# Attention and two expert layers in one kernel: where the later experts' raw weights are put and when their loads are issued, and 512-wide dummy matmuls

## The chip, the cores and the metric

The kernel runs on one core of a Trainium2 chip. The metric is the device time of one execution in microseconds (us), lower is better. Every engine of the core runs its own list of instructions in order: TensorE (PE, matmuls; PEld are its weight loads), VectorE (DVE), ScalarE (ACT), GpSimd (POOL) and SyncE (SP, which issues most transfers). They meet at semaphores.

## What is computed

A recurrence over 768 steps for 4 x 8 heads, whose output becomes 3072 rows of 384; a dense layer with leaky ReLU; then a layer of eight experts, of which each row uses at most one:

```
state = w * state + outer(k_t, v_t)              # attention, per head
y[t]  = r_t @ (state_before + outer(u * k_t, v_t))
x = leaky(y @ w_in) @ w_out                      # 3072 x 384 -> 2048 -> 384
do = x @ w_skip > 0                              # only these rows are changed
e  = argmax(x @ w_gate); gate = softmax(x @ w_gate)[e]
out[do] = x + gate * (relu(x @ w1[e]) @ w2[e])   # 384 -> 1024 -> 384
```

## The kernel before

Everything is written out by hand in one order (the recording layer keeps the order of the calls), so each engine's list is the order of the code. Each weight matrix is used as a high and a low float16 part; a product is three matmuls.

**Head.** The string SEQ names the steps of the attention, the conversion of the dense layer's weights and its first matmuls, one letter each. The letter W is a dummy matmul, 256 columns wide, that writes a bank nobody reads; there are 38 more before the string and 2 after each of the four steps at L181. After SEQ come the groups of the dense layer. They end at about 511 us of the span.

**Experts.** They are numbered 0 to 7, so the first, third and fifth are numbers 0, 2 and 4. A block is 128 rows of one expert: POOL gathers the rows (`gather`, L659), SP turns them with a DMA transpose (`turn_rows`, L673, into a tile xT, or into consts), PE runs 72 matmuls of `hidden` (L981 to L983) and 24 of `combine` (L997 to L999), DVE writes y (L1001), POOL scatters y into the output (L1004). Expert 1's first block comes first of all; then the loop L1045 goes through the experts. The numbers of rows are known only at run time, so each block after the first stands in a branch (`tc.If`), and `announce` (L1021) tells the engines' instruction fetch which way it will go. The blocks of expert 1 after its first are called block 1, 2 and 3 here.

**Weights.** An expert's split weights fill one of five slots; expert e uses slot e mod 5 of D, E, A, B, C (L681). The raw float32 weights come from HBM in eight pieces of 384 KB: four of w1 (0 to 3), four of w2 (4 to 7). `load_pieces(n)` issues the next n loads on SP (L697), always into eight places of the tile raw; `split_pieces(n)` makes the two parts of the next n pieces, ACT the high one (L190) and DVE the low one (L191), and after each, unless state["hold"] is set, loads one more piece. PIECES says how many pieces an expert's first block splits: 2, 1 and 3, at three places of it, but 2 for expert 1. So an expert splits pieces of the next one or two and loads pieces about an expert further on. The list `later` (L841) is the order of the loads.

**Expert 1's last block.** Its rows come by `fetch(e, 3)`, which stands at the head of block 1 (L1063 to L1065): on POOL and SP it comes after all that L1047 to L1050 issue, that is the fetch for expert 2, the fetch for expert 3 (into consts) and the loads that go with two splits. The matmuls of block 3 wait for this tile, xT of buffer 6.

Of the kernel before, what the change touches and what calls it, by code (L numbers as in the profile page):

```python
# [9 lines left out]
F32 = mybir.dt.float32  # L10
# [8 lines left out]
P = 128  # L19
NB, H, S, D = 4, 8, 768, 48  # L20
NT, DM, DFF = 3072, 384, 2048
E, F2 = 8, 1024
# [20 lines left out]
NW = 8  # L43
# [4 lines left out]
W0 = 30  # L48
W1 = 2
SEQ = "UqcaAWWWsDLnWWWWWWWWWWspLUqWWWWWvycNTBCWWWWWWrXLLdBqpCLtWWWWWWWWWWWWWvaueXByTlCnWWWWWWWsXWWWWrcTDpaBCWWWWWWWWWWWWWWWWWvulyXtLlBLCLqheLXLBCnXhWWWWWWWWWWWWWWWWWWWWWWWsBrtchdWWWWvCXBCepqWWWWWWWWWWWWWWWWWWWWWWWWWyluXTWWWWWrBCXBNllLCaWWWWWmLXAkvLcmuTeKmsBmcCkmdkXBsDnhkphCmmkqLpXByhCXhLkTWWWWWWWWWvBLCXLuyBCmnXBrtmtKmkLLeTmrehLCkmhvcXBlkCmKmmKLkmkaXBdmKilKmmkCmKXBCmmKlqkskXmLBmCumKkxhXBLCmmnKkXBjlmpkxmkCLKLxqmmmhXByCvxlT2KXT2BLCxXx2BLClacrLedXLfLa2q2BClXhBsx2x2lLpUCXhxB2CXBfCXyhBT2kCxxlXn2BC2xalcxrXLB2ChXxf2xl2x2s2kTq"  # L50
NB2 = 7
E0 = 1
# [8 lines left out]
def kernel(ctx: ExitStack, tc: tile.TileContext, rk, nat, wT, uN, w_in, w_out, wsg,  # L61
                         w1, w2, c_diag, c_mask, c_id48, c_f16, c_route, c_tok, out):
    nc = tc.nc
    v, act, g_, pe, sp = nc.vector, nc.scalar, nc.gpsimd, nc.tensor, nc.sync
# [14 lines left out]
    bank = [psp.tile([P, 512], F32, name=f"bank{i}") for i in range(8)]  # L79
    turns = {}  # L80
    steps = {}
    state = {"ring": 3, "loads": 0, "seq": True, "done": 0, "hold": False}
# [10 lines left out]
    wu = cst.tile([P, 2 * P], F16, name="wu")  # L93
# [5 lines left out]
    def whole():  # L99
        last_rows.clear()  # L100

    def warm(n, b, w=2 * P):

        for _ in range(n):
            whole()
            pe.matmul(bank[b][:, 256:256 + w], wu[:, :P], wu[:, :w], start=True, stop=True)


    for b in range(4):
        for o in (0, 256):  # L110
            whole()
            pe.matmul(bank[b][:, o:o + 256], wu[:, :P], wu, start=True, stop=True)
    warm(W0, 5)


    def att_load():
# [35 lines left out]
    slotA = slots.tile([P, 2, NK, DFF], F16, name="slotA")  # L152
    slotB = slots.tile([P, 2, NF, WX], F16, name="slotB")
    slotC = slots.tile([P, 2, NF, GT], F16, name="slotC")
    slotD = slots.tile([P, 2, NF, GT], F16, name="slotD")
# [22 lines left out]
    for p in range(NPAIR):  # L178
        for o in (0, 64):
            for q in range(2):  # L180
                pe.matmul(bank[q][o:o + C, p * D:(p + 1) * D], ltab[64 * q:64 * q + D, p, :], id48[64 * q:64 * q + D, :],  # L181
                          start=True, stop=True)
        warm(W1, 5)
    for q in range(2):
        act.copy(lnat[:, q].rearrange("a b c -> a (b c)"), bank[q][:, :NPAIR * D])

# [2 lines left out]
    def split(hi, lo, src, sc, eng=None):  # L189
        act.activation(hi, src, AF.Copy, scale=sc)  # L190
        (eng or v).scalar_tensor_tensor(lo, src, sc, hi, op0=ALU.mult, op1=ALU.subtract)  # L191
# [461 lines left out]
    def buf_of(e, j):  # L653
        return 3 * (e % 2) + j if j < 3 else 6
# [28 lines left out]
    def expert_piece(e, c):  # L683

        w1s, w2s = ev[e % len(ev)]
        if c < 4:
            n = F2 // 4
            sl = slice(c * n, (c + 1) * n)
            return w1[e, :, :, sl], w1s[:, 0, :, sl], w1s[:, 1, :, sl], NK
        sl = slice(2 * c - 8, 2 * c - 6)  # L690
        return w2[e, :, sl, :], w2s[:, 0, sl, :], w2s[:, 1, sl, :], 2

    def load_expert(e, c, pool, bufs):
        src, hi, lo, n = expert_piece(e, c)
        t = pool[c] if isinstance(pool, list) else pool.tile([P, 768], F32, name="wst", bufs=bufs)
        t3 = t.rearrange("p (a b) -> p a b", a=n)
        sp.dma_start(t3, src)  # L697
        return lambda eng=None: split(hi, lo, t3, SW, eng)
# [90 lines left out]
    def first_post(eng):  # L789
        turn("k")  # L790
        posts.pop(0)(eng)
# [4 lines left out]
             "q": att_load, "L": load_w, "B": conv_a, "C": conv_b, "X": conv_d,  # L796
             "l": lambda: conv_low(v), "h": lambda: conv_low(g_), "x": turn_w_out, "m": first_mm1, "M": lambda: first_mm1(g_), "2": first_mm2,
             "k": lambda: first_post(g_), "K": lambda: first_post(v), "f": first_fuse, "i": init_loads, "j": init_routing,
             "W": lambda: warm(1, 4 + (turns.get("mm", -1) + 1) % 3)}
    for x in SEQ:  # L800
        order[x]()
    state.update(ring=4, seq=False)
    turns["mm"] = 2
# [34 lines left out]
        take_logits(0, pl, 1.0 / (SX * SR))  # L838

    w_b = [raw[:, i * 768:(i + 1) * 768] for i in range(NW)]  # L840
    later = [(e, c) for e in range(2, E) for c in range(8)]  # L841
    parts = []

    def load_pieces(n):
        for _ in range(min(n, len(later))):
            parts.append(load_expert(*later.pop(0), w_b, NW))

    def split_pieces(n, more=True):
        for _ in range(min(n, len(parts))):
            parts.pop(0)()  # L850
            if more and not state["hold"]:
                load_pieces(1)
# [118 lines left out]
    def hidden(e, k, par, hset, cuts=(0, 0), between=None):  # L971
        w1s, _ = ev[e % len(ev)]
        xT = xT_b[k]
        h = h_b[par]
        for b in range(2):
            hp = hps[hset][b]
            for f in range(4):
                fs = slice((4 * b + f) * P, (4 * b + f + 1) * P)
                o = hp[:, f * P:(f + 1) * P]
                for c in range(NK):  # L980
                    pe.matmul(o, w1s[:, 0, c, fs], xT[:, c, :], start=c == 0, stop=False)  # L981
                    pe.matmul(o, w1s[:, 0, c, fs], xT[:, NK + c, :], start=False, stop=False)
                    pe.matmul(o, w1s[:, 1, c, fs], xT[:, c, :], start=False, stop=c == NK - 1)  # L983
            split_pieces(cuts[b])
            hh = h[:, 0, 4 * b:4 * b + 4, :].rearrange("p a b -> p (a b)")
            hl = h[:, 1, 4 * b:4 * b + 4, :].rearrange("p a b -> p (a b)")
            act.activation(hh, hp, AF.Relu)  # L987
            v.scalar_tensor_tensor(hl, hp, 0.0, hh, op0=ALU.max, op1=ALU.subtract)  # L988
            if between and b == 0:
                between()  # L990
# [24 lines left out]
    def fetch_ahead(e):  # L1015
        if e < E:
            fetch(e, 0)

    def announce(e, j, engines=ENGINES):

        tc.mark_branch_hint_location(f"e{e}b{j}", (rv[e] + (NT + 1023 - j * P)) >> 12, engines=engines)  # L1021
# [3 lines left out]
    def fetch_more(e):  # L1025
        with tc.If(rv[e] > P):  # L1026
            fetch(e, 1)
            with tc.If(rv[e] > 2 * P):  # L1028
                fetch(e, 2)

    def passage():
        turn_here(0, 0, bank[0])
        next(cnts)
        fetch_more(E0)
        fetch_more(0)
        state["hold"] = False
        load_pieces(2)

    state["hold"] = True
# [5 lines left out]
    for e in range(E):  # L1045
        odd = 1 if e == E0 else 0
        if e == E0:  # L1047
            fetch_more(e + 1)
            fetch_ahead(e + 2)
            split_pieces(sum(PIECES[e + 1]))  # L1050
        else:
            announce(e, 1)
            cuts = PIECES[e + 1]
            hidden(e, buf_of(e, 0), e % 2, e % 2, cuts[:2], lambda: announce(e, 1, ENGINES[:1]))
            split_pieces(cuts[2])
            announce(e, 1, ENGINES[:1])
            if e + 1 < E and e + 1 != E0:
                fetch_more(e + 1)
            combine(e, buf_of(e, 0), e % 2, idx_t[:, 0, e:e + 1], lambda: fetch_ahead(e + 2))
        st = ExitStack()  # L1060
        for j in range(1, NBLK):
            st.enter_context(tc.If(rv[e] > j * P, label=f"e{e}b{j}"))
            if j == 1:  # L1063
                with tc.If(rv[e] > 3 * P):  # L1064
                    fetch(e, 3)  # L1065
            announce(e, j + 1)
            hidden(e, buf_of(e, j), (e + j + odd) % 2, 2 if (j + odd) % 2 else e % 2, (0, 0),
                   lambda: announce(e, j + 1, ENGINES[:1]))
            announce(e, j + 1, ENGINES[:1])
            combine(e, buf_of(e, j), (e + j + odd) % 2, idx_t[:, j, e:e + 1])  # L1070
        with tc.If(rv[e] > NBLK * P, label=f"e{e}b{NBLK}"):  # L1071
            nb = (rv[e] + (P - 1)) // P
            k = NB2 - 1
            with tc.For_i(NBLK, nb, 1) as jb:
                for i in range(TPG):
                    sp.dma_start(idx_l[:, i:i + 1], idxl[i][bass.ds(jb * P + e * NT, P), :])
                v.tensor_reduce(idx_m, idx_l, op=ALU.min, axis=AX.X)
                fetch(e, 0, k, idx_m)
                hidden(e, k, e % 2, e % 2)
                combine(e, k, e % 2, idx_m)  # L1080
        st.close()  # L1081
    with tc.If(rv[E] > 0):
        later[:] = [(E0, c) for c in range(8)]
        load_pieces(8)
        idx_f = m2p.tile([P, 1], U32, name="idxf")
        v.tensor_scalar(idx_f, steps["early_i"], NT, 4 * NT, op0=ALU.is_lt, op1=ALU.mult)
        v.tensor_max(idx_f, idx_f, idx_t[:, 0, E0:E0 + 1])
        fetch(E0, 0, None, idx_f)
        split_pieces(8)
        hidden(E0, k0, 0, 2)  # L1090
        combine(E0, k0, 0, idx_f)
# [80 lines left out]
```

## Time and profile before

| | us |
|---|---|
| median of 3 runs (649.68 to 653.81) | 651.92 |
| the profiled execution | 653.15 |
| its span, first to last instruction | 651.0 |
| PE busy | 606.3 (93%) |
| DVE busy | 420.2 (65%) |
| ACT busy | 255.9 (39%) |
| POOL busy | 253.7 (39%) |
| mean granted TensorE clock | 0.987 |

A share of busy time is a mean over the whole span. PE is the engine that is nearly always at work; what it waits for decides, and only those waits of PE that a change moves can move the end. In the rows, "PEq" is PE's own sequencer, which runs branches and fetches instructions; a wait that ended with PEq ended with a branch. SPq and POOLq are transfers that SP and POOL issue: the time beside them is that of the issue, not of the transfer.

### The profile page before, as it was taken

To read this page: it belongs to the slowest core of one execution; us is meant where nothing else is said; L and a number is where in the kernel's file an instruction comes from. 1 tells how busy PE (TensorE), PEld (TensorE's weight loads), DVE (VectorE), ACT (ScalarE), POOL (GpSimd) and SP (SyncE) were. 2 spreads that over 40 slices of the span, in tenths; PEclk is the share of its full clock that TensorE was granted. 3 is DMA by queue.
4 is the path that set the end of the run, shared out by engine and by line. 5 is a ranking of instruction groups with operands and counts; after the bars stand their busy time and mean duration, and the time that the engine had idled before them with its cause. 6 is when DMAs were issued, how large, how long until landed. Compare 5 with 4: busy or idle time off the path is not lost. (4 is left out here: it accounts for less than half of the span.)

```text
span 651.0 us, 17764 instructions
## 1 busy us (share of the span) xinstructions
PE 606.3 (93%) x7198; PEld 404.4 (62%) x7198; DVE 420.2 (65%) x915; ACT 255.9 (39%) x539; POOL 253.7 (39%) x242
## 2 busy tenths in 40 slices
PE   8889988889999999999999999999998888989894
PEld 6666555556666666656666666665665666777673
DVE  6899988953379559858965961861577262553751
ACT  1226656552145235434533621441454141432540
POOL 3867764543544622534553261430024122221210
PEclk9989999999999999999999999999999899989997
DMA  8767354623624552562553242021366498397930
GB/s 262 233 186 224 95 169 138 188 66 75 161 89 127 147 187 66 135 185 78 147 150 117 65 100 87 2 74 34 110 177 193 147 224 209 94 195 200 191 135 12
DMA packets 60350, 89.04 MB, mean 137 GB/s; under 512 B 20706, under 2 KB 44224, under 8 KB 60240
## 3 DMA queue, kind: packets, MB, share of 16 engines
q1 hardware_dynamic: 56784, 81.64, 45.2%
q0 software_dynamic: 2880, 5.49, 2.8%
q8 instruction: 66, 1.08, 0.7%
q10 hardware_dynamic: 576, 0.47, 0.2%
q14 instruction: 44, 0.36, 0.2%
HBM read 68.86 MB, written 17.23 MB: 132 GB/s over the span
## 5 line engine op out<-in xcount | busy, mean ns | idle before, releaser
L476 PE MATMUL bank<-xt,slotA 128*128 128x384 f16 x384 | 125.6, 327 | 2.4 <-DVE gg L482 2.3
L478 PE MATMUL bank<-xt,slotA 128*128 128x384 f16 x384 | 125.4, 326 | 0.0
L477 PE MATMUL bank<-xt,slotA 128*128 128x384 f16 x384 | 125.3, 326 | 0.0
L504 PE MATMUL bank<-slotB,slotC 128*128 128x393 f16 (+1 forms) x336 | 110.7, 329 | 0.0
L506 PE MATMUL bank<-slotB,slotC 128*128 128x393 f16 (+1 forms) x336 | 110.5, 329 | 0.0
L505 PE MATMUL bank<-slotB,slotC 128*128 128x393 f16 (+1 forms) x336 | 110.5, 329 | 0.0
L482 DVE TENSOR_TENSOR gg<-bank,gg 128x384 f32<-128x384 f32 x128 | 70.0, 550 | 29.4 <-ACT gg L481 28.9
L481 ACT ACTIVATE gg<-bank 128x384 f32<-128x384 f32 x128 | 62.1, 490 | 48.8 <-PE bank L478 46.4
L492 DVE TENSOR_TENSOR slotC<-gg,slotC 128x384 f16<-128x384 f32 x101 | 77.7, 773 | 0.2
L297 POOL TENSOR_TENSOR dg<-cs,diag 128x512 f32<-128x512 f32 x21 | 22.2, 1058 | 131.8 <-DVE cs L290 131.8
L491 ACT CAST slotC<-gg 128x384 f16<-128x384 f32 x112 | 56.8, 508 | 22.5 <-DVE gg L482 22.5
L532 DVE SCALAR_TENSOR_TENSOR x<-bank,x 128x384 f16<-128x384 f32 x24 | 13.2, 556 | 71.4 <-ACT x L529 71.4
L269 POOL TENSOR_TENSOR raw<-raw,consts 112x512 f32<-112x512 f32 x44 | 56.9, 1318 | 0.0
L477 PEld LDWEIGHTS <-slotA 128*128 128x128 f16 x384 | 37.6, 98 | 25.1 <-issue 3.2
L478 PEld LDWEIGHTS <-slotA 128*128 128x128 f16 x384 | 37.6, 98 | 25.0 <-issue 0.2
L476 PEld LDWEIGHTS <-slotA 128*128 128x128 f16 x384 | 37.6, 98 | 23.9 <-issue 0.2
L528 ACT ACTIVATE x<-bank 128x384 f16<-128x384 f32 x24 | 11.8, 493 | 99.2 <-PE bank L506 81.2
L506 PEld LDWEIGHTS <-slotC 128*128 128x128 f16 x336 | 32.9, 98 | 22.7
L504 PEld LDWEIGHTS <-slotC 128*128 128x128 f16 x336 | 32.8, 98 | 21.9
L505 PEld LDWEIGHTS <-slotC 128*128 128x128 f16 x336 | 32.9, 98 | 20.8
L987 ACT ACTIVATE h<-bank 128x512 f16<-128x512 f32 x28 | 16.7, 597 | 71.5 <-PE bank L983 57.3
L988 DVE SCALAR_TENSOR_TENSOR h<-bank,h 128x512 f16<-128x512 f32 x28 | 19.4, 691 | 38.0 <-ACT h L987 34.0
(212 smaller groups left out, 1312.2 us busy)
## 6 DMA issues: line engine op xcount, KB each, us to landing
raw<-in_w SPq DMA_DIRECT2D x48, 384.0 KB, 6.6
raw<-in_nat SPq DMA_DIRECT2D x24, 576.0 KB, 5.4
raw<-in_rk SPq DMA_DIRECT2D x24, 448.0 KB, 4.3
xbuf<-x SPq DMA_DIRECT2D x23, 384.5 KB, 6.3
wst<-in_w_in SPq DMA_DIRECT2D x16, 384.0 KB, 7.6
wst<-in_w_out SPq DMA_DIRECT2D x16, 384.0 KB, 3.6
wst<-in_w SPq DMA_DIRECT2D x16, 384.0 KB, 5.9
out_x<-x SPq DMA_DIRECT2D x24, 192.0 KB, 1.9
```

Source lines behind the costliest of these rows:

```text
L269: eng.tensor_mul(r4[:, a], r4[:, a], tab.unsqueeze(2).broadcast_to([112, NPAIR, 2, C]))
L297: eng.tensor_mul(dg, steps.pop(("cs", i)).unsqueeze(3).broadcast_to([P, 2, NPAIR, C]), diag.unsqueeze(1).unsqueeze(1).broadcast_to([P, 2, ...
L476: pe.matmul(ph[:, :n], wh, xt[:, 0, k, t0:t0 + n], start=k == 0, stop=False)
L477: pe.matmul(ph[:, :n], wh, xt[:, 1, k, t0:t0 + n], start=False, stop=False)
L478: pe.matmul(ph[:, :n], wl, xt[:, 0, k, t0:t0 + n], start=False, stop=k == NK - 1)
L481: act.activation(gg[:, :n], ph[:, :n], AF.Copy, scale=0.01)
L482: v.tensor_max(gg[:, :n], ph[:, :n], gg[:, :n])
L491: act.copy(gT[:, 0, f, t0:t0 + n], gg[:, :n])
L492: eng.tensor_sub(gT[:, 1, f, t0:t0 + n], gg[:, :n], gT[:, 0, f, t0:t0 + n])
L504: pe.matmul(po[:, :c1 - c0], gh, w_out_s[:, 0, f, c0:c1], start=start, stop=False)
L505: pe.matmul(po[:, :c1 - c0], gh, w_out_s[:, 1, f, c0:c1], start=False, stop=False)
L506: pe.matmul(po[:, :c1 - c0], gl, w_out_s[:, 0, f, c0:c1], start=False, stop=stop)
```

## The change

Three things change.

1. A dummy matmul can be 512 wide: it reads the 256 columns of wu twice and writes a whole bank. The dummies before SEQ, those at L181 and pairs of W ahead of SEQ's first m become half as many of double width.
2. The list `later` says for each piece where it lands. Pieces 2 to 7 of expert 4 land in slot D, which expert 0 has used; all of expert 6 land in slot A, which expert 2 has used; the rest in raw. Experts 5 and 7 load (and split) pieces 2 to 7 first and 0 and 1 last.
3. Splits load nothing until expert 3's first block. Instead there are three calls of load_pieces: 10 in expert 1, 4 ahead of expert 2's first block, 8 ahead of expert 3's. As the loop goes, the loads issued in each expert's turn are:

| turn of expert | 0 | 1 | 2 | 3 | 4 | 5 |
|---|---|---|---|---|---|---|
| loads before (2 ahead of expert 0) | 6 | 2 | 6 | 6 | 6 | 4 |
| loads now (2 ahead of expert 0) | 0 | 10 | 4 | 14 | 2 | 0 |

```diff
+            if w > 2 * P:
+                pe.matmul(bank[b], wu[:, :P], wu.unsqueeze(1).broadcast_to([P, 2, 2 * P]), start=True, stop=True)
+                continue
...
-    warm(W0, 5)
+        warm(1, b, 4 * P)
+    warm(W0 // 2, 5, 4 * P)
...
-        warm(W1, 5)
+        warm(W1 // 2, 5, 4 * P)
...
-    for x in SEQ:
+    head, tail = SEQ[:SEQ.index("m")], SEQ[SEQ.index("m"):]
+    for x in head.replace("WW", "w") + tail:
...
-    later = [(e, c) for e in range(2, E) for c in range(8)]
+    rest = [2, 3, 4, 5, 6, 7, 0, 1]
+    store = {e: t.rearrange("p a b c -> p (a b c)")[:, :8 * 2 * 768].bitcast(F32) for e, t in ((4, slotD), (6, slotA))}
+    store = {e: [t[:, i * 768:(i + 1) * 768] for i in range(8)] for e, t in store.items()}
+    later = ([(e, c, w_b) for e in (2, 3) for c in range(8)] + [(4, c, w_b) for c in (0, 1)]
+             + [(4, c, store[4]) for c in range(2, 8)] + [(5, c, w_b) for c in rest]
+             + [(6, c, store[6]) for c in range(8)] + [(7, c, w_b) for c in rest])
...
         fetch_more(E0)
         fetch_more(0)
-        state["hold"] = False
         load_pieces(2)
...
             fetch_ahead(e + 2)
             split_pieces(sum(PIECES[e + 1]))
+            load_pieces(10)
         else:
             announce(e, 1)
             cuts = PIECES[e + 1]
+            if e == 2:
+                load_pieces(4)
+            if e == 3:
+                load_pieces(8)
+                state["hold"] = False
             hidden(e, buf_of(e, 0), e % 2, e % 2, cuts[:2], lambda: announce(e, 1, ENGINES[:1]))
```

What this moves on SP is seen at two places. The first is expert 1's turn, from the transpose for expert 3 (consts) to the one for expert 1's block 3 (xT_6535 before, xT_6453 now, the same buffer 6; both read its rows xg). Before:

```order
L673 DMA_TRANSPOSE consts<-consts 128x6x128
L697 DMA raw<-in_w 128x3x256 x2
L1081 COMPARE_AND_BRANCH
L1064 COMPARE_AND_BRANCH
L673 DMA_TRANSPOSE xT_6535<-xg_6534 128x6x128
L1064 UNCONDITIONAL_BRANCH x2
```

Now:

```order
L674 DMA_TRANSPOSE consts<-consts 128x6x128
L698 DMA slotD<-in_w 128x3x256 x2
L698 DMA slotD<-in_w 128x768 x4
L698 DMA raw<-in_w 128x3x256 x2
L698 DMA raw<-in_w 128x768 x2
L1093 COMPARE_AND_BRANCH
L1076 COMPARE_AND_BRANCH
L674 DMA_TRANSPOSE xT_6453<-xg_6452 128x6x128
L1076 UNCONDITIONAL_BRANCH x2
```

Ten loads stand between the two transposes where two stood. The second place is the head of expert 0's turn, between the branches of the passage and the transpose for expert 2 (xT_6520 before, xT_6438 now). Before:

```order
L697 DMA raw<-in_w 128x3x256 x2
L1021 ISA
L1168 BRANCH_PREFETCH_HINT
L697 DMA raw<-in_w 128x3x256 x2
L697 DMA raw<-in_w 128x768 x4
L673 DMA_TRANSPOSE xT_6520<-xg_6519 128x6x128
```

Now:

```order
L698 DMA raw<-in_w 128x3x256 x2
L1028 ISA
L1180 BRANCH_PREFETCH_HINT
L674 DMA_TRANSPOSE xT_6438<-xg_6437 128x6x128
L1093 COMPARE_AND_BRANCH
```

Six loads have left the place ahead of that transpose.

## Rows read from the trace of the kernel before

**Rows 1.** The page, part 1: busy us (share) and instructions of each engine.
```profile
PE 606.3 (93%) x7198; PEld 404.4 (62%) x7198; DVE 420.2 (65%) x915; ACT 255.9 (39%) x539; POOL 253.7 (39%) x242
```

**Rows 2.** Timeline of DVE, experts, lines L1001: start us, us, then the instruction.
```profile
550.68 0.62 DVE L1001 SCALAR_TENSOR_TENSOR y<-bank,xg 128x384 f32<-128x384 f32 x1 [2.60 <-PE bank L999]
...
561.23 0.62 DVE L1001 SCALAR_TENSOR_TENSOR y<-bank,xg 128x384 f32<-128x384 f32 x1 [2.60 <-PEq L1071]
...
570.01 0.61 DVE L1001 SCALAR_TENSOR_TENSOR y<-bank,xg 128x384 f32<-128x384 f32 x1
...
581.66 0.61 DVE L1001 SCALAR_TENSOR_TENSOR y<-bank,consts 128x384 f32<-128x384 f32 x1
...
589.52 0.62 DVE L1001 SCALAR_TENSOR_TENSOR y<-bank,xg 128x384 f32<-128x384 f32 x1 [2.60 <-DMA out_x<-y,idx]
...
606.40 0.62 DVE L1001 SCALAR_TENSOR_TENSOR y<-bank,xg 128x384 f32<-128x384 f32 x1
```

**Rows 3.** Waits of PE at 533, 549, 560, 569, 597, 606 us: total, times, longest.
```profile
PE bank L981 <- issue: 1.2, 1, 1.2
...
PE bank L981 <- DMA xT<-xg: 2.3, 1, 2.3
...
PE bank L981 <- PEq L1071: 0.6, 1, 0.6
...
PE bank L981 <- PEq L1081: 1.9, 1, 1.9
...
PE bank L981 <- PEq L1081: 0.7, 1, 0.7
...
PE bank L981 <- PEq L1081: 2.2, 1, 2.2
```

**Rows 4.** Windows: busy PE, PEld, DVE, ACT, POOL (instructions); clock, DMA share, GB/s.
```profile
572.00:576.00 4.00, 4.00 (x47) 4.00 (x44) 0.98 (x2) 0.77 (x2) 1.55 (x1) 0.57 1.55 265
...
642.00:651.00 9.00, 0.00 (x0) 0.00 (x0) 0.29 (x1) 0.00 (x0) 0.97 (x1) 0.62 0.04 15
```

**Rows 5.** Timeline of SP, experts: start us, us of issuing, transfer, number issued.
```profile
528.04 5.86 SPq L697 DMA_DIRECT2D raw<-in_w  x8
541.46 1.26 SPq L673 DMA_TRANSPOSE xT<-xg  x1
544.69 1.24 SPq L673 DMA_TRANSPOSE consts<-consts  x1
546.04 1.26 SPq L697 DMA_DIRECT2D raw<-in_w  x2
548.14 1.23 SPq L673 DMA_TRANSPOSE xT<-xg  x1
563.40 7.05 SPq L697 DMA_DIRECT2D raw<-in_w  x6
...
582.19 5.06 SPq L697 DMA_DIRECT2D raw<-in_w  x6
...
599.63 7.30 SPq L697 DMA_DIRECT2D raw<-in_w  x6
```

**Rows 6.** Timeline of POOL, the gathers for expert 2, expert 3 and block 3.
```profile
534.26 1.03 POOL L659 DMA_INDIRECT xg<-xbuf,idx  x1 [8.49 <-DVEq L1081]
...
538.25 1.02 POOL L659 DMA_INDIRECT consts<-xbuf,idx  x1 [1.09 <-DMA raw<-in_w]
...
544.22 1.00 POOL L659 DMA_INDIRECT xg<-xbuf,idx  x1 [4.95 <-SPq L1081]
```

**Rows 7.** Transfers issued in 528:534, 546:548, 544:546: number, KB, median us to landing.
```profile
raw<-in_w SPq DMA_DIRECT2D x8, 384.0 KB, 8.3
...
raw<-in_w SPq DMA_DIRECT2D x2, 384.0 KB, 4.9
...
xg<-xbuf,idx POOLq DMA_INDIRECT x1, 3.9
```

**Rows 8.** Window of the dummies L106 alone: PE busy (matmuls), PEld, clock, DMA, GB/s.
```profile
6.00:7.40 1.40, 1.40 (x15) 1.25 (x14) 1.00 1.10 347
```

More of the change, by code (lines that the diff above doesn't have):

```diff
@@ L105, in warm @@
             whole()
+            if w > 2 * P:
+                pe.matmul(bank[b], wu[:, :P], wu.unsqueeze(1).broadcast_to([P, 2, 2 * P]), start=True, stop=True)
+                continue
             pe.matmul(bank[b][:, 256:256 + w], wu[:, :P], wu[:, :w], start=True, stop=True)
     for b in range(4):
-        for o in (0, 256):
-            whole()
-            pe.matmul(bank[b][:, o:o + 256], wu[:, :P], wu, start=True, stop=True)
-    warm(W0, 5)
+        warm(1, b, 4 * P)
+    warm(W0 // 2, 5, 4 * P)
     def att_load():
@@ L798 @@
              "k": lambda: first_post(g_), "K": lambda: first_post(v), "f": first_fuse, "i": init_loads, "j": init_routing,
-             "W": lambda: warm(1, 4 + (turns.get("mm", -1) + 1) % 3)}
-    for x in SEQ:
+             "W": lambda: warm(1, 4 + (turns.get("mm", -1) + 1) % 3), "w": lambda: warm(1, 4, 4 * P)}
+    head, tail = SEQ[:SEQ.index("m")], SEQ[SEQ.index("m"):]
+    for x in head.replace("WW", "w") + tail:
         order[x]()
@@ L845, in load_pieces @@
         for _ in range(min(n, len(later))):
-            parts.append(load_expert(*later.pop(0), w_b, NW))
+            parts.append(load_expert(*later.pop(0), NW))
     def split_pieces(n, more=True):
@@ L1082 @@
     with tc.If(rv[E] > 0):
-        later[:] = [(E0, c) for c in range(8)]
+        later[:] = [(E0, c, w_b) for c in range(8)]
         load_pieces(8)
```

## The prediction

> **What bounds the kernel now.** I read the page's busy shares first: PE works 93% of the span, the next engine 65% [rows 1]. So time is lost or won where PE stands still, and an edit that touches no such place costs nothing. The change leaves the dense layer alone; it alters the dummies of the head and the stretch of the experts. There I read the timeline of DVE, whose y marks the end of each block. A block that waits for nothing lasts 589.52 - 581.66 = 7.86 us [rows 2]; what an interval has beyond that is loss. Then the waits of PE by windows [rows 3] say what ended the loss. Four of them matter here:
>
> - Expert 1's block 3 (y 550.68 to 561.23): PE waits 2.3 us for its tile xT.
> - End of expert 2 (y 570.01 to 581.66, 11.65 us): a wait of 1.9 us that ended with PE's own sequencer, at a branch. The remaining 11.65 - 7.86 - 1.9 = 1.9 us has its cause in the window 572 to 576: granted clock 0.57 on average, that is mostly 1.2 GHz instead of 2.4, with PE busy throughout [rows 4], right behind the wait.
> - End of expert 4, behind the y at 606.40: a wait of 2.2 us on the sequencer.
> - For comparison, the same kind of wait is 0.6 us at the end of expert 1 and 0.7 us at the end of expert 3 [rows 3].
>
> What distinguishes the long branches from the short ones is seen on SP [rows 5]: six loads are issued from 563.40 in expert 2 and six from 599.63 in expert 4, each burst running over the branch; at the ends of experts 1 (about 561) and 3 (about 597) the last loads were issued by 547.3 and 587.3, ten microseconds and more earlier. I read this as: the code behind the branch is itself a transfer and arrives late when weight loads fill the DMA engines. Expert 0 speaks half against it: eight loads from 528.04, and a wait of 1.2 us put down to issue, not to the sequencer.
>
> The chain behind the 2.3 us of block 3 is longer. The gather for expert 2 goes out at 534.26 [rows 6], among eight loads, and SP can issue its transpose only at 541.46, 7.2 us later; a gather with few loads beside it lands in 3.9 [rows 7]. SP goes on in order: the transpose for expert 3 at 544.69, two loads at 546.04, block 3's transpose at 548.14 [rows 5]. POOL's gather for block 3 itself waited 4.95 us for SP until 544.22 [rows 6]. The transpose landed when PE's wait ended, 550.6 + 2.3 = 552.9.
>
> **The dummies: nothing.** In the window 6.0 to 7.4 the dummies keep PE busy without a hole, 15 of them in 1.4 us [rows 8]; half as many of double width are the same columns. From both sides: if every merged pair saved a tenth of its length, about 0.01 us for some 80 pairs, -0.8; if each real matmul behind a wide dummy started 0.1 us later at some ten places, +1. I take 0 since no idle time lies between them.
>
> **Expert 0's six loads gone.** Its own branch needs nothing from this: the 1.2 us are issue. I count 0. What it does is to bring SP forward. The gather for expert 2 then lands at 534.26 + 3.9 = 538.2, so its transpose is issued 3.3 us sooner. The gather for expert 3, issued at 538.25, lands at about 542.2, and its transpose goes out there instead of at 544.69. By itself this would take away block 3's wait.
>
> **Expert 1's ten loads: the term that decides.** They stand on SP between the transpose for expert 3 and the one for block 3, where two stood. SP issues a load in 0.63 us (two in 1.26 [rows 5]). First load: 542.2 + 1.3 = 543.5. Tenth: issued before 550. All go through the one hardware queue of SP, and so does block 3's transpose behind them. How long it stands behind them I take from two rows. Two loads landed 4.9 us after issue; of eight loads issued in 5.86 us the median took 8.3 [rows 7]. The eighth was issued at about 533.2 and so landed at about 541.5, the first at about 528.04 + 4.9 = 532.9: 8.6 / 7 = 1.23 us per load. Ten loads then land until 543.5 + 4.9 + 9 x 1.23 = 559.5. The transpose came 1.3 us behind the last load in front of it before (546.7 + 4.9 = 551.6, then 552.9): 560.8. PE finishes block 2 at 550.6 as now, so it waits 10.2 us instead of 2.3: **+7.9**. Bounds: if the loads land as fast as they are issued, 543.5 + 4.9 + 9 x 0.63 + 1.3 = 555.4, that is +2.5; if the ten, a gather, a scatter and a transpose (4.7 MB in all) move at the 265 GB/s of the crowded window in [rows 4], 17.8 us from 544.7 on and 1.3 more, 563.8, that is +10.9. I take +7.9, nearest to the row with eight loads.
>
> A rule to weigh against this: the Trainium skill, "DMA: Bandwidth & Descriptors", section Bandwidth, gives about 358 GB/s as a core's share of HBM. By it, nine further loads of 0.393 MB take an estimated 9.9 us instead of 11.1, and the term would be +6.7; no window read here reaches that rate.
>
> After ten idle microseconds the clock falls: at the end of the kernel PE does nothing from 642 to 651, and that window has 0.62 [rows 4]. Block 3 then begins at the lower clock. The price of one such stretch is the 1.9 us measured above: **+1.9** (bounds 0 and twice that). While PE waits, nothing else suffers: ACT and DVE have only splits to do, and the loads wait for none of PE's later work. POOL's scatters come later by the same amount, with PE.
>
> **Expert 2's four loads.** They are issued ahead of its splits, right after block 3's transpose, and with the delay above they have landed before its branch. So its end becomes one like expert 1's: 1.9 to 0.6, **-1.3**, and the half clock behind it goes with the wait, **-1.9**. Bounds: 0 and -3.2.
>
> **Expert 3's fourteen, expert 4's two, expert 5's none.** At expert 4's end two loads instead of six are in front: 2.2 to 0.6, **-1.6** (bounds -1.6 and 0, since expert 3's loads may still run). Fourteen loads at 1.23 fill 17 us of expert 3's three blocks (24 us), and its rows were fetched in expert 2's turn; its end may become a long branch (+1.5) or not. I take 0, because the last block announces its branch a whole block earlier. Splitting pieces 0 and 1 of expert 7 last puts them just ahead of its first matmuls; DVE has finished such splits at the y of the block before [rows 2], where PE only begins the next: 0.
>
> **Sum.** +7.9 + 1.9 - 1.3 - 1.9 - 1.6 = **+5.0 us**. The profiled execution took 653.15 (span 651.0 and 2.15 around it), which makes 658.2; it stands 1.2 above the median 651.92, so in the measure of the median **656.9 us**, 0.8% slower. Its own range, from the bounds: 649.6 (+2.5, no clock loss) to 663.
>
> **Rivals.**
>
> 1. Block 3 is not late (chance 0.15). For it: SP and POOL reach it 3 us sooner, and a transpose might not wait for loads that stand in front of it. Then the 2.3 us stay or go, with the gains kept: -4.8 to -7.1, **647.1 down to 644.8**. It decides if the transpose lands before 552.9. Against it: loads took 8.3 instead of 4.9 us where eight stood together, and it is the same queue. The Trainium skill, "DMA: Bandwidth & Descriptors", section Queues, rings and completion order, says that each DMA engine takes descriptors in ring order but that completions may overtake one another; the first half is my forecast, the second is this rival, and no row here shows one.
> 2. The long branches are not due to the loads, or move to the end of expert 3 (0.2). For it: expert 0's branch among loads was short. Then only +7.9 + 1.9 stays, **661.7**, slower by 1.5%.
> 3. The loads hide in both places and nothing measurable moves, as all engines but PE have room (0.1): **652**. Against it: the waits above are PE's own.
>
> **Chances.** My forecast has 0.55. A difference of 1%, 6.5 us, is about what a measurement of this kernel can tell from no change. Slower by more than that is above 658.4: a third of the forecast (the upper half of the bounds of the ten loads) and rival 2, 0.39. Faster is below 645.4: only rival 1 with its whole gain, 0.06. The rest, 0.55, is within 1%. The range that holds 8 in 10 leaves out the best of rival 1 and the ends of the forecast: 647 to 663.
>
> **What would show it.** In the profile after: the wait of PE for xT before block 3 of expert 1 about 10 us instead of 2.3, with SP's ten loads from about 543.5 and block 3's transpose issued after 550; the granted clock low behind it; the waits at the ends of experts 2 and 4 at 0.6 to 0.7, and the stretch behind expert 2 at full clock. A wait under 3 us at block 3 makes the forecast wrong; long branches at experts 2 and 4, or a new one at the end of 3, put rival 2 in its place.

## The result and the profile after

The changed kernel takes 661.13 us (median of 4 runs, 658.57 to 661.30), the kernel before beside it 650.93 (4 runs, 649.68 to 653.81). The ratio is 1.0118, 95% interval 1.0084 to 1.0151: slower by 1.2%. The forecast was 656.9, in a range of 647 to 663. The profiled execution took 661.19 us with a span of 659.0, 8.0 more than before.

The page's shares look as they did [rows 1]:

```profile
PE 608.3 (92%) x7116; PEld 395.1 (60%) x7116; DVE 418.5 (64%) x915; ACT 255.6 (39%) x539; POOL 253.3 (38%) x242
```

Where the 8 us lie is read from the y of DVE, one at the end of each block. These are the lines that answer to [rows 2] (line numbers up to some L840 are one higher now, those of the experts seven to twelve):

```profile
547.74 0.62 DVE L1008 SCALAR_TENSOR_TENSOR y<-bank,xg 128x384 f32<-128x384 f32 x1 [2.60 <-PE bank L1006]
...
567.76 0.62 DVE L1008 SCALAR_TENSOR_TENSOR y<-bank,xg 128x384 f32<-128x384 f32 x1 [2.60 <-PEq L1083]
577.92 0.61 DVE L1008 SCALAR_TENSOR_TENSOR y<-bank,xg 128x384 f32<-128x384 f32 x1
586.34 0.61 DVE L1008 SCALAR_TENSOR_TENSOR y<-bank,consts 128x384 f32<-128x384 f32 x1
...
602.08 0.62 DVE L1008 SCALAR_TENSOR_TENSOR y<-bank,xg 128x384 f32<-128x384 f32 x1 [2.60 <-PE bank L1006]
615.29 0.62 DVE L1008 SCALAR_TENSOR_TENSOR y<-bank,xg 128x384 f32<-128x384 f32 x1 [1.02 <-PE bank L1006]
```

Block 3 of expert 1 (547.74 to 567.76) takes 20.0 us; it took 10.55 [rows 2]. Expert 2 has one block; it and the first block of expert 3 (567.76 to 586.34), with expert 2's end between them, take 18.6 instead of 20.4. From 602.08 to 615.29, over expert 3's end and through expert 4's one block, it is 13.2 instead of 9.0. The waits of PE in the windows 546:559, 567:569, 576:579, 600:604, 605:609 and 614:617, which answer to [rows 3], name what ended them:

```profile
PE bank L988 <- DMA xT<-xg: 10.3, 1, 10.3
...
PE bank L988 <- PEq L1083: 0.7, 1, 0.7
...
PE bank L988 <- PEq L1093: 0.4, 1, 0.4
...
PE bank L988 <- PEq L1093: 1.3, 1, 1.3
...
PE bank L988 <- issue: 2.1, 1, 2.1
```

The first is the forecast's main term: PE stands 10.3 us before block 3, where it stood 2.3 [rows 3], and waits for the transposed rows. Then come the ends of expert 1 (0.7), expert 2 (0.4, was 1.9) and expert 3 (1.3, was 0.7), and a wait of 2.1 inside expert 4's block for which this view names no cause ("issue"). The end of expert 4, the window 614:617, reads 0.4 like expert 2's; it was 2.2.

What SP did around block 3 is in its timeline (start, us of issuing, transfer, number):

```profile
540.13 1.22 SPq L674 DMA_TRANSPOSE consts<-consts  x1
541.47 3.35 SPq L698 DMA_DIRECT2D slotD<-in_w  x6
544.91 2.97 SPq L698 DMA_DIRECT2D raw<-in_w  x4
548.47 2.69 SPq L674 DMA_TRANSPOSE xT<-xg  x1
```

Ten loads, then the transpose at 548.47, which landed when PE's wait ended, at 558.0. The trace also has the packets in which the transfers move, and they show the order: on SP's queue the first packet of the loads starts at 543.0 and the first of the transpose (its packets are of 256 bytes, a load's of 1,024 or 3,072) at 554.9, 11.9 us later. In that window (543:554.9) the queue moves 3.67 of the ten loads' 3.93 MB and nothing of the transpose (packets, MB, share of the engines' time):

```profile
q1 hardware_dynamic: 2359, 3.67, 94.4%
```

And these windows show the engines and the clock in and behind the wait, and in expert 4 (busy time of PE, PEld, DVE, ACT, POOL; granted clock; DMA share; GB/s):

```profile
547.60:551.00 3.40, 0.04 (x1) 0.00 (x0) 0.62 (x1) 0.00 (x0) 0.99 (x1) 1.00 0.99 343
551.00:558.00 7.00, 0.02 (x1) 0.02 (x1) 0.00 (x0) 0.00 (x0) 0.00 (x0) 0.50 1.08 310
558.00:561.30 3.30, 3.30 (x31) 3.24 (x32) 0.00 (x0) 0.00 (x0) 0.00 (x0) 0.50 1.07 371
609.10:612.50 3.40, 3.40 (x20) 2.02 (x18) 1.61 (x3) 2.28 (x4) 1.04 (x1) 0.50 0.68 217
```

Nothing computes in the second window; the DMA engines are full throughout. There the granted clock stands at half (1.2 GHz instead of 2.4), with PE idle in it and in the window ahead, and block 3 does its first 3.3 us of work at that level. The last window is a second stretch of half clock, behind the 2.1 us in expert 4.

### The profile page after: what moved, and what is told of

Read it like the earlier page. It is cut to its first block, busy times and chain, and to the rows that moved or that the text cites. A ratio compares the mean times of both kernels' runs of the same rounds, so it can differ in the third digit from the quotient of the medians.

```text
span 659.0 us, 17597 instructions
## 1 busy us (share of the span) xinstructions
PE 608.3 (92%) x7116; PEld 395.1 (60%) x7116; DVE 418.5 (64%) x915; ACT 255.6 (39%) x539; POOL 253.3 (38%) x242
## 5 line engine op out<-in xcount | busy, mean ns | idle before, releaser
L479 PE MATMUL bank<-xt,slotA 128*128 128x384 f16 x384 | 125.2, 326 | 0.0
L533 DVE SCALAR_TENSOR_TENSOR x<-bank,x 128x384 f16<-128x384 f32 x24 | 13.2, 556 | 75.9 <-ACT x L530 73.8
L529 ACT ACTIVATE x<-bank 128x384 f16<-128x384 f32 x24 | 11.8, 493 | 100.1 <-PE bank L507 81.8
```

The source lines that it names most:

```text
L479: pe.matmul(ph[:, :n], wl, xt[:, 0, k, t0:t0 + n], start=False, stop=k == NK - 1)
```

## The experiments

Twelve runs. The time of one block, from one y to the next, is the unit in which they are compared. All intervals below are differences of the times of y in the profiled execution of each kernel; "experts" is the time from the first y to the end of the span. "2's end" is expert 2's block and the first of expert 3, "4's end" the first block of expert 5 and "5's end" that of expert 6, each with the wait ahead of it. A name with "again" is a second execution of the same program (fourteen_again of fourteen_in_expert1).

| kernel | first y | expert 1 block 3 | 2's end | 3's end, 4's middle | 4's end | 5's end | experts |
|---|---|---|---|---|---|---|---|
| before | 523.8 | 10.5 | 20.4 | 9.0 | 10.2 | 8.8 | 127.2 |
| after | 519.5 | 20.0 | 18.6 | 13.2 | 9.5 | 8.8 | 139.5 |
| after_again | 523.4 | 20.9 | 18.2 | 11.3 | 9.4 | 8.8 | 136.2 |
| dummies_only | 524.9 | 8.3 | 18.8 | 9.3 | 9.6 | 12.1 | 126.7 |
| dummies_only_again | 522.5 | 13.3 | 17.3 | 9.8 | 8.5 | 10.9 | 128.6 |
| loads_only | 525.5 | 20.7 | 18.4 | 9.2 | 9.2 | 8.8 | 136.3 |
| six_loads | 524.7 | 13.9 | 18.3 | 13.7 | 9.3 | 8.8 | 131.9 |
| fetch_first | 519.8 | 7.9 | 19.5 | 11.3 | 8.5 | 8.8 | 125.7 |
| fetch_first_again | 524.5 | 7.9 | 19.4 | 11.4 | 9.3 | 8.8 | 125.2 |
| late_expert7 | 522.9 | 7.9 | 20.7 | 8.9 | 8.2 | 11.8 | 125.9 |
| late_expert7_again | 521.2 | 7.9 | 20.0 | 9.0 | 9.0 | 12.0 | 126.3 |
| fourteen_in_expert1 | 523.8 | 7.9 | 19.5 | 14.0 | 8.2 | 11.6 | 129.6 |
| fourteen_again | 522.7 | 7.9 | 19.8 | 8.9 | 9.1 | 13.5 | 127.2 |
| before_fetch_first | 524.0 | 9.2 | 19.0 | 9.6 | 11.8 | 8.8 | 126.3 |

**The two parts apart.** dummies_only is the kernel before with the dummies of the change; loads_only is the changed kernel with the old dummies:

```diff
 # dummies_only, on the kernel before
...
-    warm(W0, 5)
+        warm(1, b, 4 * P)
+    warm(W0 // 2, 5, 4 * P)
...
 # loads_only, on the changed kernel: those lines the other way round
```

> The kernel before with the 512-wide dummies alone; no load is moved. Two theories of the 2.5 us by which the changed kernel is ahead at 85 us of the span. First (the dummies): 256-wide dummies use up PE's instruction list twice as fast, so PE ran dry once in the head, a wait of 2.1 us put down to issue at 15 us of the span; with the wide ones this wait is gone. Expected: no issue wait over 0.5 us of PE before 20 us, the first matmul of the group behind 84.9 us about 2.4 us sooner, and the end 2 to 4 us sooner (a ratio of 0.994 to 0.997). Second (chance of the execution): the wait at 15 us stays in a new execution of either kernel now and then, the ratio is 1.000 and the head ends where it did.

> The changed kernel with the old 256-wide dummies: only the landing places and the times of the loads are changed. If the loads alone cost the time, the wait of PE for xT before block 3 of expert 1 is about 10.3 us as in the changed kernel and the time is 10 to 13 us over the kernel before (1.015 to 1.02), more than the changed kernel's own difference by the 2 to 3 us of the dummies. If the dummies had a part in the loss (a different clock in the expert stretch, for example), the difference is smaller than the changed kernel's.

Measured: dummies_only 652.93 us against 653.41, ratio 0.9995 (0.9963 to 1.0028). loads_only 662.86, ratio 1.0139 (1.0079 to 1.0200); span 661.8. The loads are the whole slowdown; the ratio is a little under the 1.015 to 1.02 that was expected, and its interval takes that in. The dummies move the time by nothing that can be measured, and the 2 to 4 us expected of them did not come. In loads_only's trace PE waits before block 3 as in the changed kernel (window 551:564), and at the head it has a wait put down to issue (window 12:22), as the kernel before has for 2.1 us:

```profile
PE bank L393 <- issue: 3.3, 1, 3.3
...
PE bank L990 <- DMA xT<-xg: 10.7, 1, 10.7
```

**Expert 1's order and number of loads.** fetch_first lets block 3's gather and transpose go ahead of expert 3's fetch and of the ten loads; nothing else is changed. (The rows of expert 2's one block are fetched earlier, in expert 0's turn; what `fetch_more` adds at this place is for further blocks of expert 2, which has none.) six_loads leaves block 3 behind the loads but puts six there instead of ten, and the four others ahead of expert 2.

```diff
 # fetch_first, on the changed kernel, at the head of expert 1's turn
+            with tc.If(rv[e] > 3 * P):
+                fetch(e, 3)
...
-            if j == 1:
+            if j == 1 and e != E0:
 # six_loads, on the changed kernel
-            load_pieces(10)
+            load_pieces(6)
...
-                load_pieces(4)
+                load_pieces(8)
```

> The changed kernel, but the fetch for expert 1's block 3 (gather and transpose) stands ahead of the fetch for expert 2 and so ahead of the ten loads on SP; the same loads, bytes and slots. Theory (order in SP's queue): the transpose no longer stands behind the ten loads, lands before 545 us, and PE's wait of 10.3 us before block 3 goes to under 1 us; with it goes the stretch at half clock: 11 to 12 us less than the changed kernel, that is 647 to 651 us, at or under the kernel before. Rival (crowding: ten loads in flight slow every transfer, whatever the order, or they hold PE by way of the slots): the wait stays at 5 us or more.

> The changed kernel with 6 loads instead of 10 in expert 1's turn and 8 instead of 4 ahead of expert 2's first block. Theory (each load ahead of the transpose holds it by 1.2 us): the wait before block 3 is 10.3 - 4 x 1.2 = 5.5 us, 4.5 to 6.5. Rival (the wait comes from one load that is itself late, or from the slot D that has to be free): the wait is the same 10 us, or nothing.

> fetch_first a second time. Theory A: the block of expert 3's end and expert 4's middle again 11 to 12 us (11.3), expert 2's end again 2.2 to 2.6 us of branch. Rival B: the block anywhere from 9 to 14, the branch anywhere from 0.5 to 2.5. No wait for the transposed rows ahead of block 3 under both.

Measured: fetch_first 650.19 us (10 runs), ratio to the kernel before 0.9962 (0.9929 to 0.9994), the only version here whose interval lies below 1. six_loads 657.73, ratio 1.0060 (1.0024 to 1.0096). In fetch_first no wait is left before block 3, in both executions, and the block takes the 7.9 us of one that waits for nothing, with the ten loads now behind its transpose. In six_loads the wait before block 3 (window 551:557) is

```profile
PE bank L988 <- DMA xT<-xg: 4.1, 1, 4.1
```

So four loads fewer take 10.3 - 4.1 = 6.2 us from the wait, somewhat more than the 3.8 to 5.8 expected. Not all of it is the loads': the transpose itself, from its first packet to its landing, took 3.1 us behind ten and 1.9 behind six. The packets give the price of a load without that. In six_loads the first of the loads starts at 547.6 and the first of the transpose at 553.8, and between them (window 547.6:553.8) SP's queue moves almost six loads:

```profile
q1 hardware_dynamic: 1345, 2.31, 103.2%
```

That is 6.2 us for six loads, against 11.9, 11.2 and 11.6 for ten in after, after_again and loads_only: 1.0 to 1.2 us for each. The cause is shown from two sides: with the transpose in front of the loads the wait is gone, and with fewer loads in front of the transpose it shrinks. fetch_first's transpose was through before the first load started, so the run does not tell a wait in the queue from crowding by loads in flight; the packets do, since the transpose's first one starts only when nearly all bytes in front of it have gone. What fetch_first gains over the changed kernel in the stretch of the experts, 139.5 and 136.2 down to 125.7 and 125.2, is 10.5 to 14.3 us.

**Which waits belong to loads in flight.** fetch_first still has waits of PE at the end of expert 2 (2.4, and 1.8 in its second execution, where theory A wanted 2.2 to 2.6), at the end of expert 3 (1.6, 1.4) and in the middle of expert 4 (1.3, 1.5). late_expert7 takes the eight last loads out of the turns of experts 3 and 4 (six and two) and issues them behind expert 4's block; by PIECES it also splits two pieces fewer in expert 5 and two more in expert 6. fourteen_in_expert1 also moves expert 2's four to expert 1.

```diff
 # late_expert7, on fetch_first
-PIECES = [(1, 0, 1), (2, 1, 3), (2, 0, 0)] + 5 * [(2, 1, 3)] + [(0, 0, 0)]
+PIECES = [(1, 0, 1), (2, 1, 3), (2, 0, 0)] + 3 * [(2, 1, 3)] + [(2, 1, 1), (2, 2, 4), (0, 0, 0)]
...
-                state["hold"] = False
...
+            if e == 4:
+                load_pieces(8)
 # fourteen_in_expert1, on late_expert7
-            load_pieces(10)
+            load_pieces(14)
...
-            if e == 2:
-                load_pieces(4)
```

> The run fetch_first with one more change: the eight loads for the seventh expert's raw pieces that expert 3 issued (slot A's eight, or those behind it in the list) no longer go out together with the others there; expert 3 issues only the eight for the freed slot, and the last eight go out after expert 4's block. Theory A (bulk loads in flight make TensorE's branch at an expert's end, and the move to the next instructions in the middle of expert 4, late): the end of expert 3 goes from 1.58 us to 0.7 to 1.0, the issue wait in the middle of expert 4 from 1.32 to under 0.3, and the half-clock stretch there, if any, is gone; 1.5 to 3 us less than fetch_first, about 643 in the profile's span and a ratio to the kernel before of 0.992. The end of expert 2 (2.44 in fetch_first) stays, since the loads ahead of it stay. Rival B (these waits come from the announcement of the branch, which is now only one block ahead, not from loads): both stay within 0.4 us of 1.58 and 1.32, and the time stays at fetch_first's 0.996.

> late_expert7 with the four loads that expert 2's turn issued put with expert 1's ten, so that fourteen go out there, behind the fetch of block 3, and none in expert 2's turn. Theory A (loads in flight at an expert's end lengthen its branch): fourteen loads at about 1.4 us each take until some 20 us after their start near 541 us, about 561, well ahead of expert 2's end near 572; so that end goes from 2.44 us to about 0.6, with the 3.4 us of half clock behind it gone (worth up to 1.7): 2 to 3.5 us less than late_expert7, ratio about 0.988. Rival B (the length of the branch has nothing to do with loads in flight): the end stays at 1.9 to 2.5 us and the time with late_expert7's.

> late_expert7 a second time (eight loads in expert 3's turn). Theory A: the block again about 9 us (8.9) and expert 5's end again about 2.4 us, since the eight late loads are in flight there. Rival B: the block anywhere from 9 to 14 and expert 5's end anywhere from 0.6 to 2.5.

> fourteen_in_expert1 a second time, which has the same eight loads in expert 3's turn as late_expert7 but showed 4.1 us of branch at expert 3's end and 2.4 us in expert 4's middle. Theory A (loads in flight decide): since it differs from late_expert7 only up to expert 2, the 4.1 us shouldn't recur: block about 9 us. Rival B: block anywhere from 9 to 14. Rival C (the place of the instructions in memory, which is the program's own, decides): 4.1 us and 13.9 us again.

Measured: late_expert7 651.11 us, ratio 0.9980 (0.9948 to 1.0012); fourteen_in_expert1 650.52, ratio 0.9969 (0.9930 to 1.0008). Neither is the gain over fetch_first that theory A wanted. In the traces the first half of A holds: with eight loads instead of fourteen, expert 3's end and expert 4's middle take 8.9 and 9.0 us instead of 11.3 and 11.4, in both executions, and no wait is left in expert 4's middle. Then expert 5's end, where the late loads are now in flight, takes 11.8 and 12.0 instead of 8.8. These are late_expert7's waits of PE at the ends of experts 2, 3 and 5 (windows 567:570, 595:597, 620:624):

```profile
PE bank L988 <- PEq L1096: 2.1, 1, 2.1
...
PE bank L988 <- PEq L1096: 0.6, 1, 0.6
...
PE bank L988 <- DMA raw<-in_w: 2.4, 1, 2.4
```

2.4 us are gained at expert 3's end and 3.0 lost at expert 5's. That the stall went with the loads is not shown by this: dummies_only has 12.1 and 10.9 us at expert 5's end with the loads of the kernel before, which has 8.8. fourteen_in_expert1 spoils the simple rule further. With the same eight loads in expert 3's turn its first execution had the longest wait of all at expert 3's end (window 594:600) and its second the usual short one (window 593:595):

```profile
PE bank L988 <- PEq L1094: 4.1, 1, 4.1
```

```profile
PE bank L988 <- PEq L1094: 0.6, 1, 0.6
```

(The 2.4 us that the expectation of fourteen_again puts in expert 4's middle stand at 533 us, in expert 1; expert 4's middle has no such wait.) Expert 2's end, with the loads ahead of it moved earlier, was 0.5 in the first execution, but followed by 1.8 of issue some three microseconds later, and 2.2 in the second. So part of this belongs to the single execution.

**The order of the fetch alone.** before_fetch_first is the kernel before with fetch_first's edit.

> The kernel before with only the order of the fetch changed: the gather and transposing load for block 3 go ahead of the ones for expert 2 and of the loads. Theory A (the transposing load waits behind the queued raw loads on the DMA engines, and that alone made the 2.3 us wait ahead of block 3 in the kernel before): the wait is gone, and what lies after it is 2 to 2.5 us earlier, ratio 0.9965. Rival B (the wait was taken up by slack elsewhere, or expert 2's fetch, now second, comes late instead): a wait of 1 to 2 us appears ahead of expert 2's block, and the ratio is 0.999 to 1.001.

Measured: 652.40 us against 652.95, ratio 0.9997 (0.9965 to 1.0029). PE's wait before block 3 (window 550:553) fell from 2.3 [rows 3] to

```profile
PE bank L981 <- DMA xT<-xg: 0.9, 1, 0.9
```

That is 1.4 us less, 0.2% of the time, and smaller than the interval. The run tells neither theory from the other in time. In the trace the transpose goes out 1.1 us sooner than before (547.0, not 548.1), since it still has to wait for its gather; its packets start 1.8 us sooner (548.9, not 550.7), with no loads in front. With two loads the place in the order matters little.

**The same programs once more.** after_again and dummies_only_again are the changed kernel and dummies_only without an edit, for what in their waits recurs.

> The changed kernel itself a second time, for the spread of its waits. In the runs so far the block that holds expert 3's end and expert 4's middle took, from one weighted sum of y to the next, 13.2 us in the changed kernel, 9.2, 11.3 and 13.7 in three others with the same fourteen loads in expert 3's turn, and 8.9 and 13.9 in two with eight loads there; 9.0 to 9.6 with six. Theory A (the stall belongs to the program: fourteen loads in flight make the instructions late): 12.5 to 14 again, with about 2 us of issue wait in expert 4's middle. Rival B (where the stall falls is the single execution's own): anything from 9 to 14. Under both the wait ahead of block 3 is 10 to 10.7 us again. The first sum of y stood at 519.5 and stood at 523 to 525.5 in most other kernels: theory A (wide dummies save it) 519 to 520, rival B 522 to 525.

> dummies_only a second time. Its loads are those of the kernel before, six of them in flight over expert 2's end, and yet the branch there waited 0.4 us, while ACT's second relu of expert 2's first block came about 1.4 us late; the two blocks took 10.2 and 8.5 us, as in the changed kernel (10.2 and 8.0 to 8.4), where the kernel before has 8.8 and 11.6. Theory A (what is late at expert 2's end follows the program as laid out, not the loads in flight): 10.2 and 8.5 again, branch 0.4. Rival B (it falls out either way in single executions): 8.8 to 9.2 and 10.2 to 11.8, branch about 2. Expert 5's end, 2.4 us in the first look against 0.6 in the kernel before with the same loads: 2.4 under A, anything from 0.6 to 2.4 under B.

Measured: after_again 661.89 us, span 659.6. Its waits before block 3, at the end of expert 3 and in expert 4's middle (windows 549:561, 604:608, 609:612):

```profile
PE bank L988 <- DMA xT<-xg: 10.3, 1, 10.3
...
PE bank L988 <- PEq L1093: 2.0, 1, 2.0
...
PE bank L988 <- issue: 0.8, 1, 0.8
```

The 10.3 recur to a tenth. The stall of expert 3's end and expert 4's middle recurs in the sum of its two waits (3.4, then 2.8), but spread otherwise, and with no half clock behind it: 11.3 us for the block, not 13.2. The first y stood at 523.4, so the 4.3 us by which the first execution was ahead there were its own: it lacks a wait of 2.0 us for DVE's x at about 512 us that the kernel before has, and that is 1.9 in after_again.

dummies_only_again 653.23 us, and it is the run that decides about expert 2's end. Its loads are those of the kernel before. SP issues six of them in expert 2 (its timeline: start, us of issuing, transfer, number):

```profile
565.13 7.05 SPq L698 DMA_DIRECT2D raw<-in_w  x6
```

From there to past the expert's end the DMA engines move 247 GB/s (window; columns as above):

```profile
565.10:572.20 7.10, 6.71 (x76) 4.91 (x73) 6.29 (x9) 5.48 (x8) 2.35 (x2) 1.00 0.80 247
```

And PE's wait at that end (window 570:573; the window of expert 4's end, 605:607, has the same line) is

```profile
PE bank L983 <- PEq L1083: 0.4, 1, 0.4
```

It is 0.4 us at both places in the first execution too. The kernel before had 1.9 and 2.2 with the same loads. So the long branch at these two places is gone with the dummies alone, and also with the loads alone (0.4 and 0.5 in loads_only). Loads in flight don't suffice to make it long. Two other things did not recur as theory A wanted: expert 2's block took 8.8 us, not 10.2, with ACT's second relu on time, and the end of expert 5 waited 1.9 us, not 2.4. And before block 3, with the same two loads in front as in the kernel before, PE waited 3.4 us here and not at all in dummies_only, where the kernel before has 2.3; the 13.3 us of that block are this wait and a stretch at half clock behind it (553.6 to 557.0).

**What the long branches have in common.** The trace also has the packets of the queue that the profile calls instruction, 16 KB each. In the fourteen profiles 20 waits of PE in the experts lasted over 1.2 us and ended with PEq (1.3 to 4.1 us). Each of them ended 1.7 to 2.2 us after the end of such a packet, however long the wait was. In 19 the packet had started 0.3 to 2.0 us before the wait; in the longest, the 4.1, it started 0.6 us into it. The packets took 0.9 to 1.5 us, and over the whole span their median is 1.0. The clearest case is the end of expert 6 in loads_only, where no load is left (wait of PE in 642:645, packets of all queues in 641:644.4):

```profile
PE bank L990 <- PEq L1095: 1.3, 1, 1.3
...
DMA packets 2, 0.02 MB, mean 7 GB/s; under 512 B 0, under 2 KB 0, under 8 KB 0
...
q8 instruction: 1, 0.02, 1.8%
...
q14 instruction: 1, 0.01, 0.7%
```

The 16 KB packet runs from 641.5 to 642.5 and the wait ends at 644.4, with nothing but code on the DMA engines. So these waits are most likely waits for code, and a branch can be long without a load in flight. This is read from the times alone; no run moved such a packet on purpose.

## Why the prediction was right or wrong

Term by term, from the two executions of the changed kernel against the profiled one of the kernel before:

| step | forecast | after | after_again |
|---|---|---|---|
| up to the first y (dummies, head) | 0 | -4.3 | -0.4 |
| block 3, wait and clock | +7.9 + 1.9 | +9.5 | +10.4 |
| expert 2's end | -1.3 - 1.9 | -1.8 | -2.2 |
| expert 3's end, expert 4's middle | 0 | +4.2 | +2.3 |
| expert 4's end | -1.6 | -0.7 | -0.8 |
| all else | 0 | +1.1 | -0.7 |
| sum | +5.0 | +8.0 | +8.6 |

- **Expert 1's ten loads: right in mechanism and size.** Wait 10.3 in both executions, forecast 10.2. In after_again PE was ready at 550.0 and the transpose had landed at 560.2, forecast 550.6 and 560.8; in the first execution both came 2.8 to 3.0 us sooner (547.6 and 558.0), with the whole stretch. The price of a load, 1.23 in the forecast, is 1.1 to 1.2 by the packets of ten. The growth of 8.0 is against one execution; with two loads in front the wait was 2.3, 0 and 3.4. By the Trainium skill's rule, "DMA: Bandwidth & Descriptors", section Bandwidth (about 358 GB/s for a core), ten loads take an estimated 11.0 us; the packets of ten took 11.2 to 11.9 here, between that and the forecast's 12.3 (ten times 1.23).
- **The half clock behind it: right.** Of the 9.5 and 10.4 us, 8.0 and 7.9 are the wait; 1.5 and 2.5 are left for a restart at half clock, forecast 1.9. PE worked at that level for 3.3 us in the first execution and 5.4 in the second (560.2 to 565.6), which costs half of it, 1.7 and 2.7.
- **Expert 2's end: the wait went as forecast, the reason was wrong.** It fell from 1.9 to 0.4, and the half clock behind it went too. But dummies_only does the same twice with the old loads in flight. The comparison on which the step rested, long branches at experts 2 and 4 with loads just issued, short ones at 1 and 3 without, was of two cases each in one execution. fetch_first has the counter-example in its own trace: at expert 1's end the DMA engines move 386 GB/s (window 555.8:556.7) and PE waits 0.7. And expert 2's block and the one behind it together gained only 1.8 to 2.2 of the 3.2: the block ahead of that end grew by 1.4, because ACT's second relu came 1.3 us late there, for no reason that the profile shows. Over the fourteen executions one of the two mostly comes: in five the relu is late (the block takes 10.2 us) and the branch takes 0.4; in seven the relu is late by 0.4 at most (8.8 to 9.2) and the branch takes 1.8 to 2.6; two have neither.
- **Expert 4's end: the wait, not the time.** 2.2 to 0.4 was forecast as 2.2 to 0.6, but the block lost only 0.7 to 0.8 us; in it the first relu of expert 5 came late and the second right behind it. Why is not shown.
- **Expert 3's fourteen loads: the step that failed.** I took 0, "because the last block announces its branch a whole block earlier", with +1.5 in reserve. It was +4.2 and +2.3: a longer branch (1.3 and 2.0 instead of 0.7), a wait in the middle of expert 4 (2.1 and 0.8) that I had not looked for, and once a stretch at half clock behind it. Over all executions with fourteen loads there (after, after_again, loads_only, six_loads, fetch_first and its second) this block takes 9.2 to 13.7, mean 11.7; over the eight with six or eight loads 8.9 to 14.0, mean 9.8. That is a tendency of 2 us, with exceptions on both sides; loads_only, with fourteen, lost nothing here. So the step that put this place at 0 failed, and what makes it long is not shown to be the number of loads.
- **The dummies: 0 in time, as forecast, but not in the trace.** A wait of PE at 15 us of the span, put down to issue, is there in all executions with narrow dummies (before 2.1, before_fetch_first 2.2, loads_only 3.3) and in none of the eleven with wide ones. It is moved rather than gone: eight of the eleven have a wait put down to issue at 23 to 25 us, of 0.3 to 2.1 (fetch_first_again 2.1, dummies_only_again 1.7). All of 0.4 us and more, narrow and wide, ended 1.2 to 1.6 us after the end of a 16 KB instruction packet. My argument, no hole between the dummies, did not look at what comes behind them. The first y comes at 519.5 to 524.9, mean 522.7, with wide dummies and at 523.8 to 525.5, mean 524.4, with narrow ones: some 1.7 us, below what dummies_only's interval (0.9963 to 1.0028) can tell. The forecast's lower bound was also too small: by [rows 8] a tenth of a pair is 0.019 us, 80 of them -1.5 and not -0.8.

The sum came nearer than its parts. In the stretch of the experts the first execution lost 12.3 us (139.5 against 127.2), and 4.3 came back ahead of it by luck. The result lies in the part, slower by more than 1%, to which the prediction gave 0.39. The range's upper end, 663, is given without its terms; with every bound at its worst (+10.9, +3.8, no gain, +1.5) it would be 668.

Rival 2 (661.7: the long branches are not due to the loads, or move to expert 3's end) came nearest to the time, and half of it is what the runs show. It is right that loads in flight alone do not make those two branches long, and that a stall came up at expert 3's end. It is wrong in that the waits of experts 2 and 4 did go. Rival 1 is out: the transpose does stand behind the loads in front of it. Rival 3 is out with it.

What stays open is what decides whether an expert's end costs 0.4 or 2 us, that is, by the times above, when the code's packet comes. Loads in flight are neither enough (0.4 in dummies_only) nor needed (1.3 in loads_only). The same loads gave 0.4 in one program and 1.9 in another, and one program gave 4.1 and 0.6 in two executions. The programs differ in their instructions far ahead of that place (17,764 in the kernel before, 17,600 with the dummies alone); whether that is what matters was not tried.

## What to carry to other kernels

Before moving bulk loads into a gap, look at what the same queue has to carry right behind them: here ten loads of 384 KB cost nothing by their volume and 8 us by standing in front of one small transpose, and putting that one first gave it all back, and 0.4% (0.1 to 0.7) beyond the kernel before. A cause read from two long and two short waits of one execution is a guess: profile the same program twice, and one that alters only an unrelated part, before a term rests on it.

## What the runs showed of the hardware

- A DMA transpose on SP's queue moves behind the loads issued before it: its first packet starts 11.2 to 11.9 us after the first of ten loads' (after, after_again, loads_only), 6.2 after the first of six, 2.2 after the first of two (before, dummies_only_again). TensorE's wait for it was 10.3 to 10.7, 4.1, and 0 to 3.4 us; with ten loads behind it there was none.
- TensorE waits 1.3 to 4.1 us at some branches; all 20 such waits ended 1.7 to 2.2 us after the end of a 16 KB instruction packet, one of them with no load in flight (loads_only, 1.3). Their length differs between programs with the same loads (0.4 and 1.9) and between executions of one program (4.1 and 0.6). Waits at the head, at 15 us in three of three executions with narrow dummies and at 23 to 25 us in eight of eleven with wide ones, ended 1.2 to 1.6 us after such a packet where they reached 0.4 us.
- Behind a wait of about 2 us the granted clock sometimes falls to half and sometimes doesn't: in late_expert7 the 2.1 us at expert 2's end were followed by it, in fetch_first the 2.4 us at the same place were not. The windows behind the two waits:

```profile
570.00:575.00 5.00, 5.00 (x64) 5.00 (x62) 2.21 (x3) 1.33 (x2) 1.46 (x1) 0.66 0.71 130
```

```profile
566.00:570.00 4.00, 2.75 (x50) 2.76 (x51) 1.82 (x2) 0.49 (x1) 2.42 (x2) 1.00 0.69 133
```

The columns are those of the windows above; the seventh, 0.66 against 1.00, is the granted clock.
